# Posting one unit's small loads between two weight pieces, copying y by halves, and moving one y behind two products

## The chip, the cores and the metric

The kernel runs on one core of a Trainium2 chip. The metric is the device time of one execution in microseconds, as the median of several runs. Five engines of the core work side by side: TensorE (PE in the profile, with its weight loads as PEld), VectorE (DVE), ScalarE (ACT), GpSimd (POOL) and SyncE (SP), which here does nothing but issue DMAs, in order.

## The reference

A Mamba-2 state-space layer (4 sequences, 8 heads, 768 steps, head width 32, state width 16), and then a feed-forward layer with SiLU over its 3072 rows of 256 channels (2048 hidden):

```python
def _attn_ref(x, a, B, C):
    ...                                              # for each chunk c of the sequence
    cum = np.cumsum(la, axis=-1)                     # la = log(clip(a))
    L = np.exp(cum[:, :, :, None] - cum[:, :, None, :]) * causal
    CB = np.einsum('bhin,bhjn->bhij', Cc, Bc)
    M = CB * L
    y_intra = np.einsum('bhij,bhjd->bhid', M, xc)
    y_inter = np.einsum('bhin,bhnd->bhid', Cc, state) * decay_to_i[:, :, :, None]
    y[:, :, sl] = y_intra + y_inter
    Bx = np.einsum('bhjn,bhjd->bhjnd', Bc, xc) * decay_from_j[:, :, :, None, None]
    state = decay_full[:, :, None, None] * state + np.sum(Bx, axis=2)

def _moe_ref(x, w_in, w_out):
    h = x @ w_in
    g = h * (1.0 / (1.0 + np.exp(-h)))
    return (g @ w_out).astype(np.float32)
```

The weights `w_in` and `w_out` reach the kernel as 64-bit floats and are converted to 32 bits on the chip.

## The kernel before

The work is cut into 12 units of 256 steps (3 for each sequence). For each unit the scan makes y, which is copied to `XM`; then come the products with `w_in`, SiLU, and the products with `w_out`. Two units are taken together in the products with `w_out`, and from unit 4 on in those with `w_in` too, by a scheme that needs seven products in place of eight.

A unit needs these loads: `pa` and `ab` (two layouts of a), `tbc` (C, and for some units B, in another layout), `bn` (B) and `xt` (x). They are issued by SyncE, in this order:

```python
    def load_unit(u):
        load_pa(u, nc.sync)
        if 0 < u < UPB:
            load_n(u, 1, nc.sync)          # C of unit 1 and 2, two DMAs, 64 bytes a packet
        else:
            load_t(u, 0, nc.sync)
            load_t(u, 1, nc.sync)
        load_ab(u, nc.sync)                # four DMAs
        load_n(u, 0, nc.sync)              # B, two DMAs
        load_x(u, nc.sync)
```

The weights come in 16 pieces of 512 KB, eight of `w_in` and eight of `w_out`, through seven raw buffers. The first seven are posted at the start; `mark` is a DMA of one word that holds SyncE's queue until an earlier piece has landed:

```python
    for n in range(3):
        load_w(n, nc.sync)
    load_n(1, 0, nc.sync)
    load_n(1, 1, nc.sync)
    load_x(1, nc.sync)

    mark = const.tile([1, RAW], U32, name="mark")
    for n in range(3, RAW):                # RAW = 7
        if n > 4:
            nc.sync.dma_start(out=mark[:, n:n + 1], in_=raw[n - 2][0:1, 0, 0, 0:1])
        load_w(n, nc.sync)
```

Each piece is converted in two steps, "size" on ScalarE and "bits" on VectorE and GpSimd; the second one posts the piece seven further on:

```python
    def w_size(n):
        ...
            nc.scalar.activation(u, raw[n][:, :, :, 1].bitcast(FP32), AF.Abs)
            nc.scalar.activation(v, raw[n][:, :, :, 0], AF.Copy, scale=2.0 ** -51, bias=2.0)

    def w_bits(n, parts=1):
        ...                                # three operations on VectorE (L174, L176, L178)
                nc.gpsimd.tensor_tensor(out=dst[:, :, fs].bitcast(U32), ...)      # L182
        if n + RAW < len(W):
            load_w(n + RAW, nc.sync)
```

In the scan, `f_TP` transposes B and C of units 1 and 2 on TensorE (L355), `f_E` makes the decays E from `ab` on VectorE (L303), `f_B` multiplies B with E on GpSimd (`BT`, B-tilde, L340), `f_G` makes the products with x (L389) and CB (L404), `f_M` makes M on VectorE (L415), `f_Y` makes y on TensorE (L458, L467), and `f_X` copies it out of PSUM:

```python
    def f_X(u):
        XM[u] = xmp.tile([128, 4, 128], FP32, name="XM")
        nc.scalar.activation(XM[u], DP.pop(u)[:, :, 0:128], AF.Copy)

    def f_s1(g, j):                        # products with w_in and SiLU, for 256 hidden channels
        ...
        xm = XM[g].rearrange("p (w c) t -> p w (c t)", w=2)
        hp = ps_h.tile([128, 2, UT], FP32, name="hp")          # one of three buffers
        for i in range(2):
            f = 2 * j + i
            for kc in range(KC):           # KC = 2: the two halves of the channels of y
                nc.tensor.matmul(out=hp[:, i], lhsT=w_in_sb[:, kc, f * 128:(f + 1) * 128],
                                 rhs=xm[:, kc], start=(kc == 0), stop=(kc == KC - 1))
        nc.scalar.activation(GTS[g][:, :, j], hp, AF.Silu)
```

The order of the first units ("s6" is the size step of piece 6, "b6" its bits step; E, D, T, C, G, Y are parts of the scan of unit 2):

```python
    f_Y(0); f_Ab(1, 1); f_X(0); w_size(2); w_bits(1)
    load_unit(2)
    f_s1(0, 0)
    ...
    f_Y(1); f_X(1); w_size(5)
    f_s1(0, 3)
    steps = ((1, 0, "b5 s6"), (1, 1, "b6 s7"), (1, 2, "b7 s8"), (1, 3, "b8"), (0, 4, "E D"),
             (1, 4, ""), (0, 5, "T C s9"), (1, 5, "b9 s10"), (0, 6, "G"), (1, 6, "b10 s11"),
             (0, 7, "Y b11 s12"), (1, 7, "b12 s13"))
    for g, j, todo in steps:
        f_s1(g, j)
        w_steps(todo)
    load_unit(3)
```

And the stage in which unit 3's products with `w_in` run beside the scans of units 4 and 5 and the products with `w_out` of units 0 and 1 (`f_s2(n)`: n of these):

```python
    for j in range(8):
        f_s1(3, j)
        scan_piece(4, j, ("TE", "DCS", "G", "YS", "", "", "", ""))
        scan_piece(5, j, ("", "", "T", "E", "DCS", "G", "YS", ""))    # y of unit 5 at j = 6
        ...
        f_s2(2 if j in (5, 6) else 4)
```

Of the kernel before, what the change touches and what calls it, by code (L numbers as in the profile page):

```python
# [9 lines left out]
U32 = mybir.dt.uint32  # L10
BF16 = mybir.dt.bfloat16
AF = mybir.ActivationFunctionType
# [9 lines left out]
def kernel(  # L22
# [22 lines left out]
    nc = tc.nc  # L45
# [12 lines left out]
    const = ctx.enter_context(tc.tile_pool(name="const", bufs=1))  # L58
# [20 lines left out]
    def at(u):  # L79
        return u // UPB, u % UPB * UT  # L80

    def load_pa(u, q):

        b, t0 = at(u)
        pa[u] = loads.tile([128, UT], FP32, name="pa")
        q.dma_start(out=pa[u], in_=bass.AP(tensor=a.tensor, offset=a.offset + b * H * S + t0,
                                           ap=[[S, H], [0, N], [1, UT]]))

    def load_ab(u, q):

        b, t0 = at(u)
        ab[u] = loads2.tile([128, 2, H, Q], FP32, name="ab")
        for t in range(4):
            k, c = divmod(t, 2)
            q.dma_start(out=ab[u][64 * c:64 * c + 64, k],  # L95
                        in_=bass.AP(tensor=a.tensor, offset=a.offset + b * H * S + t0 + t * Q,
                                    ap=[[0, 64], [S, H], [1, Q]]))

    def load_n(u, i, q):

        b, t0 = at(u)
        if i == 0:
            t = bn[u] = loads.tile([128, 2, H, N], FP32, name="bn")
        else:
            t = tbc[u] = loads.tile([128, 2, 2, 8, N], FP32, name="tbc")[:, 0]
        for k in range(2):
            q.dma_start(out=t[:, k], in_=(B, C)[i][b, :, t0 + 128 * k:t0 + 128 * k + 128].rearrange("h p n -> p h n"))  # L107

    def load_t(u, i, q):

        b, t0 = at(u)
        if i == 0:
            tbc[u] = loads.tile([128, 2, 2, 8, N], FP32, name="tbc")
        for g in range(4):
            q.dma_start(out=tbc[u][32 * g:32 * g + 32, i],
                        in_=(B, C)[i][b, 2 * g:2 * g + 2, t0:t0 + UT].rearrange("e (t r) n -> t e r n", r=8))

    def load_x(u, q):
        b, t0 = at(u)
        xt[u] = loads.tile([128, 2, H, D], FP32, name="xt")  # L120
        for k in range(2):
            q.dma_start(out=xt[u][:, k], in_=x[b, :, t0 + 128 * k:t0 + 128 * k + 128].rearrange("h p d -> p h d"))

    def load_unit(u):
        load_pa(u, nc.sync)
        if 0 < u < UPB:
            load_n(u, 1, nc.sync)
        else:
            load_t(u, 0, nc.sync)
            load_t(u, 1, nc.sync)  # L130
        load_ab(u, nc.sync)
        load_n(u, 0, nc.sync)
        load_x(u, nc.sync)

    w_in_sb = const.tile([128, KC, d_ff], FP32, name="w_in_sb")
    w_out_sb = const.tile([128, NF, d_model], FP32, name="w_out_sb")
# [4 lines left out]
    RAW = 7  # L141
    raw, wu, wv = {}, {}, {}
# [7 lines left out]
    def load_w(n, q):  # L150
        src, dst = w_piece(n)
        if src.dtype == FP32:
            q.dma_start(out=dst, in_=src)
            return
        t = raw[n] = rawp.tile([128, 2, WF, 2], U32, name="raw")
        q.dma_start(out=t.rearrange("p k f two -> p k (f two)"), in_=src.bitcast(U32))
# [47 lines left out]
    load_n(1, 1, nc.sync)  # L204
    load_x(1, nc.sync)

    mark = const.tile([1, RAW], U32, name="mark")
    for n in range(3, RAW):
        if n > 4:
            nc.sync.dma_start(out=mark[:, n:n + 1], in_=raw[n - 2][0:1, 0, 0, 0:1])  # L210
        load_w(n, nc.sync)


# [57 lines left out]
    E, M, BT, BH, CT, CE, CW, PFX, ST, SM, DP, XM, GTS, BX = ({} for _ in range(14))  # L271
# [23 lines left out]
    def f_P(u):  # L295
        f_P0(u)
        f_P1(u)
# [34 lines left out]
    def f_E(u):  # L332
        f_E0(u, 0, 1)
        f_E1(u, 0, 2)
        f_E1(u, 1, 2)

    def f_B(u, engine=nc.gpsimd):

        BT[u] = sc.tile([128, 2, H, N], FP32, name="BT")
        engine.tensor_tensor(out=BT[u], in0=bn[u], in1=E[u][:, :, :, Q - 1:Q].to_broadcast([128, 2, H, N]),  # L340
                                op=ALU.mult)

    def f_T(u, i):

        t = (BH, CT)[i][u] = sc.tile([128, UT], FP32, name=("bh", "ct")[i])
        nc.vector.transpose(out=t.rearrange("p (t r) -> p r t", r=8), in_=tbc[u][:, i].rearrange("p e r n -> p r e n"))
        if i == 1:
            tbc.pop(u)

    def f_TP(u):  # L350

        tp = ps_o.tile([128, 512], FP32, name="o_ps")
        for i, t in enumerate((bn[u], tbc.pop(u))):
            for k in range(2):
                nc.tensor.transpose(out=tp[:, 256 * i + 128 * k:256 * i + 128 * k + 128],  # L355
                                    in_=t[:, k].rearrange("p h n -> p (h n)"), identity=ident)
        BH[u] = sc.tile([128, UT], FP32, name="bh")
        nc.scalar.activation(BH[u], tp[:, 0:256], AF.Copy)
        CT[u] = tp[:, 256:512]

    def f_T2(u, e):

        if e == 0:
            CE[u] = sc.tile([128, 2, UT], FP32, name="ce")
        nc.scalar.activation(CE[u][:, e], CT[u], AF.Copy, scale=par[:, e:e + 1])

    def f_C(u):

        CW[u] = sc.tile([128, UT], FP32, name="cw")
        engine = nc.vector if 0 < u < UPB else nc.gpsimd  # L370
        engine.tensor_tensor(out=CW[u].rearrange("p (c t) -> p c t", t=Q),
                             in0=CT.pop(u).rearrange("p (c t) -> p c t", t=Q), in1=PFX[u][:, :, 1:], op=ALU.mult)
# [68 lines left out]
    def f_GMD(u):  # L441
        f_G(u)
        f_S(u)
        f_SM(u)
        for k in range(2):
            f_M(u, k)
# [26 lines left out]
    def f_X(u):  # L473

        XM[u] = xmp.tile([128, 4, 128], FP32, name="XM")
        nc.scalar.activation(XM[u], DP.pop(u)[:, :, 0:128], AF.Copy)

    def new_g():

        return gpool.tile([128, NF, UT], FP32, name="gT").rearrange("p (k j) t -> p k j t", k=2)  # L480


    def f_s1(g, j):
        if j == 0:
            GTS[g] = new_g()
        xm = XM[g].rearrange("p (w c) t -> p w (c t)", w=2)
        hp = ps_h.tile([128, 2, UT], FP32, name="hp")
        for i in range(2):
            f = 2 * j + i
            for kc in range(KC):  # L490
# [3 lines that stand above are left out]
        if j == 7:  # L494
            XM.pop(g)
# [138 lines left out]
    def f_s2(n):  # L634
        for _ in range(n):
            if S2 and next(S2[0], S2) is S2:
                S2.pop(0)
                f_s2(1)
# [100 lines left out]
    def scan_piece(u, j, plan):  # L739
        for what in plan[j]:  # L740
            if what == "E":
                f_P(u)
                f_E(u)
            elif what == "T":
                if u < UPB:
                    f_TP(u)
                else:
                    f_T(u, 0)
                    f_T(u, 1)
                f_T2(u, 0)  # L750
                f_T2(u, 1)
            elif what == "t":
                f_T(u, 0)
                f_T(u, 1)
            elif what == "B":
                f_B(u)
                f_C(u)
            elif what == "D":
                f_B(u)
            elif what == "C":  # L760
                f_C(u)
            elif what == "S":
                f_SW(len(SW))
            elif what == "G":
                f_GMD(u)
            elif what == "Y":
                f_Y(u)
                f_X(u)
# [48 lines left out]
    f_X(0)  # L817
    w_size(2)
    w_bits(1)
    load_unit(2)  # L820
    f_s1(0, 0)
    f_Ek(1, 0)
    f_TP(1)
# [40 lines left out]
    def outputs(todo):  # L864
        for what in todo:
            what()
# [29 lines left out]
    for j in range(8):  # L896
        waiting, PEND[:] = PEND[:], []
        f_s1(3, j)
        scan_piece(4, j, ("TE", "DCS", "G", "YS", "", "", "", ""))
        scan_piece(5, j, ("", "", "T", "E", "DCS", "G", "YS", ""))  # L900
        scan_piece(6, j, ("",) * 7 + ("t",))
        if j == 7:
            for i in range(4):
                f_XT(2, i)

        f_s2(2 if j in (5, 6) else 4)
        if j == 3:
            f_SO(3)
        outputs(waiting)
        if j == 5:  # L910
            f_T1(1, 0)
            f_T1(1, 1)
            f_TS(1, 3, 0)
        if j in (2, 5):
            load_unit(6 + j // 3)
# [67 lines left out]
```

## Time and profile before

| | |
|---|---|
| time, median of 3 runs | 353.75 us (352.82 to 354.04) |
| profiled execution: span | 353.3 us |
| PE busy | 343.8 us, 97% of the span |
| VectorE, ScalarE, GpSimd busy | 58%, 46%, 32% |
| DMA | 42.79 MB, mean 121 GB/s |

The page's second part cuts the span into 40 slices of 8.83 us; a digit is the busy share in tenths:

```
PE   8979999999999999999999999999999999999995
DVE  6997879978586663553664563564452232234821
ACT  2567487233323645454645445544545454453100
DMA  6986895699649398958179956057404237522202
```

PE is at 9 in nearly every slice. VectorE and the DMA engines are busy early, while the weights are loaded and converted, and later have room. A busy engine in such a row does not say what the others wait for: that is read from the order of instructions in a stage. A row of the timeline gives start and length in us, the engine and the line of the kernel, what is written and read, the shape, and the count; "SPq" stands for a DMA's issue by SyncE, whose length holds any time that the issue was held up. One product in the program (32-bit, 128x256) shows as two records of PE.

### The profile page before, as it was taken

To read this page: it belongs to the slowest core of one execution; us is meant where nothing else is said; L and a number is where in the kernel's file an instruction comes from. 1 tells how busy PE (TensorE), PEld (TensorE's weight loads), DVE (VectorE), ACT (ScalarE), POOL (GpSimd) and SP (SyncE) were. 2 spreads that over 40 slices of the span, in tenths; PEclk is the share of its full clock that TensorE was granted. 3 is DMA by queue.
4 is the path that set the end of the run, shared out by engine and by line. 5 is a ranking of instruction groups with operands and counts; after the bars stand their busy time and mean duration, and the time that the engine had idled before them with its cause. 6 is when DMAs were issued, how large, how long until landed. Compare 5 with 4: busy or idle time off the path is not lost.

```text
span 353.3 us, 8349 instructions
## 1 busy us (share of the span) xinstructions
PE 343.8 (97%) x3308; PEld 287.5 (81%) x3308; DVE 204.4 (58%) x408; ACT 162.0 (46%) x394; POOL 111.5 (32%) x137
## 2 busy tenths in 40 slices
PE   8979999999999999999999999999999999999995
PEld 3658778888888888888888888888888888888883
DVE  6997879978586663553664563564652232234821
ACT  2567487233323645454645445544545454453100
POOL 4344335554085041244041244041234112051200
PEclk9999999999999999999999999999999999999999
DMA  6986895699649398958179956057404237522202
GB/s 107 225 243 161 174 371 108 125 194 210 132 99 154 81 185 164 184 104 147 32 146 185 172 98 105 16 98 143 92 2 74 51 61 142 90 46 38 36 4 46
DMA packets 117376, 42.79 MB, mean 121 GB/s; under 512 B 102488, under 2 KB 109144, under 8 KB 117336
## 3 DMA queue, kind: packets, MB, share of 16 engines
q1 hardware_dynamic: 110328, 25.67, 34.7%
q0 software_dynamic: 4464, 16.25, 24.9%
q10 hardware_dynamic: 2544, 0.33, 0.6%
q8 instruction: 26, 0.43, 0.6%
q14 instruction: 14, 0.11, 0.1%
HBM read 22.83 MB, written 3.15 MB: 74 GB/s over the span
## 4 chain that ended last, share of the span: by engine, by line
PE 75%; DVE 9%; DMA 8%; SPq 5%; issue 2%; ACT 0%; ACTq 0%; DVEq 0%
PE o_ps L627 32%; PE hp L682 28%; PE hp L491 4%; PE hp L627 3%; DMA out_dram<-ot 2%; DMA ab<-in_a_dram 2%; SPq L95 2%; PE o_ps L613 2%; PE gy L467 2%; DVE E L303 1%; DVE E L415 1%; DMA raw<-in_moe_w_out_dram 1%; SPq L107 1%; PE gy L458 1%; DMA gT<-in_a_dram 1%
## 5 line engine op out<-in xcount | busy, mean ns | idle before, releaser
L685 DVE TENSOR_TENSOR gT<-hp,p 128x256 f32<-128x256 f32 x64 | 26.9, 420 | 73.8 <-ACT p L696 37.9
L491 PE MATMUL hp<-XM,w_in_sb 128*128 128x256 f32 x256 | 59.6, 382 | 2.0 <-POOL w_in_sb L182 2.0
L627 PE MATMUL o_ps<-gT,w_out_sb 128*128 128x256 f32 x240 | 60.4, 379 | 0.0
L688 ACT ACTIVATE gT<-gT 128x256 f32<-128x256 f32 x96 | 39.7, 414 | 44.0 <-DVE gT L685 43.9
L491 PEld LDWEIGHTS hp<-XM,w_in_sb 128*128 128x128 f32 x256 | 47.9, 190 | 10.0 <-POOL w_in_sb L182 3.3
L682 PE MATMUL hp<-raw 128*128 128x256 f32 x192 | 52.7, 380 | 0.0
L544 POOL TENSOR_TENSOR ps<-ps 128x256 f32<-128x256 f32 x35 | 29.2, 835 | 72.3 <-ACT ps L574 71.0
L627 PEld LDWEIGHTS o_ps<-gT,w_out_sb 128*128 128x128 f32 x240 | 45.4, 190 | 6.3
L539 POOL DMA_DIRECT2D gT<-gT x31 | 27.4, 921 | 64.9 <-PE hp L682 22.3
L682 PEld LDWEIGHTS hp<-raw 128*128 128x128 f32 x192 | 36.2, 190 | 5.4 <-POOL ps L544 0.6
L696 ACT ACTIVATE p<-hp 128x256 f32<-128x256 f32 x64 | 24.5, 383 | 27.5 <-PE hp L682 26.1
L685 DVE TENSOR_TENSOR gT<-hp,u 128x256 f32<-128x256 f32 x32 | 13.6, 425 | 39.3 <-PE hp L682 39.3
L682 PE MATMUL hp<-XM,w_in_sb 128*128 128x256 f32 x128 | 34.1, 389 | 0.0
L493 ACT ACTIVATE gT<-hp 128x512 f32<-128x512 f32 x32 | 19.0, 594 | 28.3 <-PE hp L491 28.2
L682 PEld LDWEIGHTS hp<-XM,w_in_sb 128*128 128x128 f32 x128 | 23.3, 190 | 4.3 <-issue 1.0
L303 DVE TENSOR_TENSOR_SCAN E<-ab,diag 128x256 f32<-128x256 f32 (+1 forms) x32 | 25.6, 842 | 0.4
L574 ACT ACTIVATE ps<-o_ps 128x256 f32<-128x256 f32 x38 | 14.4, 382 | 23.9 <-PE o_ps L627 22.2
L340 POOL TENSOR_TENSOR BT<-bn,E 128x256 f32<-128x256 f32 x12 | 9.0, 748 | 50.2 <-DVE E L303 48.9
L627 PE MATMUL o_ps<-gT,wu 128*128 128x256 f32 x88 | 22.4, 380 | 0.0
L627 PE MATMUL o_ps<-gT,wv 128*128 128x256 f32 x88 | 22.2, 380 | 0.0
L627 PE MATMUL o_ps<-gT,raw 128*128 128x256 f32 x80 | 20.6, 382 | 0.0
L682 PE MATMUL hp<-raw,w_in_sb 128*128 128x256 f32 x64 | 19.1, 380 | 0.0
(125 smaller groups left out, 518.7 us busy)
## 6 DMA issues: line engine op xcount, KB each, us to landing
gT<-gT POOLq DMA_DIRECT2D x31, 512.0 KB, 6.0
ab<-in_a_dram SPq DMA_DIRECT2D x40, 128.0 KB, 3.9
raw<-in_moe_w_in_dram SPq DMA_DIRECT2D x8, 512.0 KB, 6.3
raw<-in_moe_w_out_dram SPq DMA_DIRECT2D x8, 512.0 KB, 6.5
xt<-in_x_dram SPq DMA_DIRECT2D x24, 128.0 KB, 5.7
out_dram<-ot SPq DMA_DIRECT2D x92, 32.0 KB, 2.5
bn<-in_B_dram SPq DMA_DIRECT2D x22, 64.0 KB, 4.8
tbc<-in_C_dram SPq DMA_DIRECT2D x40, 32.0 KB, 1.8
```

What stands on the lines that cost most here:

```text
L303: nc.vector.tensor_tensor_scan(out=E[u].rearrange("p k h t -> p (k h t)")[:, Q * g0:Q * (g0 + n)], data0=t.rearrange("p g t -> p (g t)"), ...
L340: engine.tensor_tensor(out=BT[u], in0=bn[u], in1=E[u][:, :, :, Q - 1:Q].to_broadcast([128, 2, H, N]), op=ALU.mult)
L491: nc.tensor.matmul(out=hp[:, i], lhsT=w_in_sb[:, kc, f * 128:(f + 1) * 128], rhs=xm[:, kc], start=(kc == 0), stop=(kc == KC - 1))
L493: nc.scalar.activation(GTS[g][:, :, j], hp, AF.Silu)
L539: nc.gpsimd.dma_start(out=o[:, js], in_=a[:, js], accum_op=ALU.add)
L544: engine.tensor_tensor(out=o, in0=p, in1=q, op=op)
L574: nc.scalar.activation(pn, on, AF.Copy)
L627: nc.tensor.matmul(out=o, lhsT=w(j), rhs=g()[:, j], start=(j == 0), stop=(j == last))
L682: nc.tensor.matmul(out=o, lhsT=w, rhs=x_, start=start, stop=True, skip_group_check=True)
L685: nc.vector.tensor_tensor(out=o, in0=p, in1=q, op=ALU.add)
L688: nc.scalar.activation(o, i, AF.Silu)
L696: nc.scalar.activation(o, i, AF.Copy)
```

## The change

Three things change. First, the loads of unit 2 are split: `pa`, C and B (`load_bc`) are posted between weight pieces 5 and 6, in place of a `mark`, and `ab` and x (`load_ax`) where all of the unit's loads stood before. It is meant to have B and C of unit 2 there before TensorE asks for them. As a consequence B stands ahead of `ab` in all units from 2 on. Second, y of units 0 and 1 is copied in two halves, so that the products with the first half of the channels may begin before the second half is copied. Third, two products with `w_out` are moved ahead of unit 5's y, so that they fill the time in which M of that unit is awaited.

```diff
-    def load_unit(u):
+    def load_bc(u):
         load_pa(u, nc.sync)
         if 0 < u < UPB:
             load_n(u, 1, nc.sync)
         else:
             load_t(u, 0, nc.sync)
             load_t(u, 1, nc.sync)
+        load_n(u, 0, nc.sync)
+
+    def load_ax(u):
         load_ab(u, nc.sync)
-        load_n(u, 0, nc.sync)
         load_x(u, nc.sync)
+
+    def load_unit(u):
+        load_bc(u)
+        load_ax(u)
...
-    mark = const.tile([1, RAW], U32, name="mark")
+    mark = const.tile([1, 1], U32, name="mark")
     for n in range(3, RAW):
-        if n > 4:
-            nc.sync.dma_start(out=mark[:, n:n + 1], in_=raw[n - 2][0:1, 0, 0, 0:1])
+        if n == 5:
+            nc.sync.dma_start(out=mark, in_=raw[3][0:1, 0, 0, 0:1])
+        if n == 6:
+            load_bc(2)
         load_w(n, nc.sync)
...
         XM[u] = xmp.tile([128, 4, 128], FP32, name="XM")
-        nc.scalar.activation(XM[u], DP.pop(u)[:, :, 0:128], AF.Copy)
+        y = DP.pop(u)
+        n = 2 if u < 2 else 4
+        for i in range(0, 4, n):
+            nc.scalar.activation(XM[u][:, i:i + n], y[:, i:i + n, 0:128], AF.Copy)
...
-    load_unit(2)
+    load_ax(2)
...
         f_s1(3, j)
+        if j == 6:
+            f_s2(2)
         scan_piece(4, j, ("TE", "DCS", "G", "YS", "", "", "", ""))
...
-        f_s2(2 if j in (5, 6) else 4)
+        f_s2((4, 4, 4, 4, 4, 2, 0, 4)[j])
```

## The prediction

> **What bounds the kernel now.** I read the page first. Section 1 puts the matmul engine at the top, and the granted clock (PEclk, 9 in all 40 slices) leaves nothing to explain there:
>
> ```profile
> PE 343.8 (97%) x3308; PEld 287.5 (81%) x3308; DVE 204.4 (58%) x408; ACT 162.0 (46%) x394; POOL 111.5 (32%) x137
> ```
>
> Second, busy time by stage (I chose the borders). The columns after the stretch's length are busy us (and instructions) of PE, PEld, DVE, ACT, POOL, then the clock, the DMA share and GB/s:
>
> ```profile
> 14.00:52.00 38.00, 35.10 (x490) 28.18 (x476) 31.45 (x54) 24.97 (x49) 15.23 (x14) 1.00 0.82 223
> 52.00:96.00 44.00, 44.00 (x433) 37.40 (x432) 35.67 (x57) 17.48 (x36) 18.76 (x17) 1.00 0.83 156
> 96.00:114.00 18.00, 17.76 (x286) 14.98 (x282) 14.39 (x22) 5.71 (x13) 11.95 (x12) 1.00 0.71 127
> 114.00:300.00 186.00, 186.00 (x1712) 158.49 (x1711) 90.81 (x214) 93.61 (x250) 52.55 (x70) 1.00 0.59 109
> ```
>
> PE has no idle time from 52 to 96 us and from 114 to 300. So nothing that the change does can shorten those stretches; at most it can keep or spoil them. What can be won lies in 14 to 52 us (38.00 - 35.10 = 2.90 us idle) and in 96 to 114 (0.24).
>
> Third, PE in order of time, around each place that the change speaks of. In brackets is the idle time ahead of a group and what ended it:
>
> ```profile
> 26.21 14.08 PE L491 MATMUL hp<-XM,w_in_sb 128*128 128x256 f32 x64 [0.73 <-POOL w_in_sb L182]
> 40.59 0.75 PE L355 MATMUL o_ps<-ident,bn 128*128 128x128 f32 x2 [0.30 <-DMA bn<-in_B_dram]
> 41.18 0.38 PE L355 MATMUL o_ps<-ident,tbc 128*128 128x128 f32 x2
> ...
> 50.15 0.69 PE L458 MATMUL gy<-cw,sm 32*64 32x64 f32 x32 [0.50 <-DVE E L415]
> ...
> 107.96 0.69 PE L458 MATMUL gy<-cw,sm 32*64 32x64 f32 x32 [0.24 <-DVE E L415]
> ```
>
> The first wait is for unit 2's B, which lands too late for the transposes; the second for unit 2's M = CB*L, the third for unit 5's. The B wait is larger than its 0.30. In unit 1 the same transposes started at 17.20 and those of C at 17.42, 0.22 us apart; here 40.59 and 41.18, 0.59 apart, because the second half of B landed later still. So 0.30 + 0.37 = 0.67 us.
>
> Fourth, the sync engine's queue, which shows why B and unit 2's M are late:
>
> ```profile
> 24.31 0.41 SPq L156 DMA_DIRECT2D raw<-in_moe_w_out_dram  x1
> 24.78 0.68 SPq L86 DMA_DIRECT2D pa<-in_a_dram  x1
> 25.50 4.97 SPq L107 DMA_DIRECT2D tbc<-in_C_dram  x2
> 30.52 5.94 SPq L95 DMA_DIRECT2D ab<-in_a_dram  x4
> 36.50 1.25 SPq L107 DMA_DIRECT2D bn<-in_B_dram  x2
> 37.79 2.82 SPq L122 DMA_DIRECT2D xt<-in_x_dram  x2
> 40.71 4.13 SPq L156 DMA_DIRECT2D raw<-in_moe_w_out_dram  x7
> ```
>
> B is issued at 36.50 because C and `ab` sit in front of it for 4.97 and 5.94 us, and the next weight piece (number 9) can't be issued before 40.71. The chain of waits then runs from that piece to the 0.50 us on PE:
>
> ```profile
> 35.82 4.50 DMA ab<-in_a_dram
> 40.71 5.00 DMA raw<-in_moe_w_out_dram
> 48.80 1.21 DVE E L415 x2
> ```
>
> Piece 9 lands at 45.71; ScalarE and VectorE convert it first (VectorE 46.49 to 47.97), and only then do unit 2's state and M come, ending at 50.01.
>
> **What the Trainium skill says.** "DMA: Bandwidth & Descriptors", section "Queues, rings and completion order": a sync-engine DMA is spread over rings, and each of the 16 engines takes descriptors in ring order. The queue above agrees: after four weight pieces (issued from 22.04 on), C's two issues take 4.97 us, where B's two take 1.25, so what is posted first is served first. The same page, "Why small descriptors are slow (HBM only)": each packet has a fixed cost. C and B come in packets of 64 bytes and the weights in pieces of 2 KB, and the page's slices from 26.5 to 44 us, where those loads run, show 161 and 174 GB/s against 371 in the slice from 44 to 53, which is weights alone for the most part. "VectorE: DVE Perf Modes", section on the TRN2 errata: a ScalarE copy out of PSUM has a fixed part beside the part per element. The trace agrees: 128x512 takes 0.60 us, 128x256 0.38, so two halves are not free.
>
> **The change part by part.**
> (1) Unit 2's `pa`, C and B are posted between pieces 5 and 6, ahead of pieces 6, 7 and 8, instead of after 8; `ab` and x stay behind 8. One gate (piece 6 waiting for piece 4 through `mark`) goes. B is then issued some ten microseconds sooner (from 36.5 to about 25 or 27) and lands well ahead of 40. Removed: 0.67 us of PE.
> (2) With 1.25 us of B gone from in front of it, and without the stretch around 33 to 35 us where the queue was stuck on `ab` and the DMA engines had nearly nothing to do (0.25 and 0.28 busy in 32 to 34 and 34 to 36), piece 9 should be issued around 38 and land around 43 instead of 45.7. VectorE then converts it by about 46, M is done near 48, and PE comes to unit 2's y at 50.15 - 0.50 - 0.67 = 48.98. Removed: 0.50. It needs M 50.01 - 48.98 = 1.0 us sooner, so piece 9 has to land at least 1.0 us sooner; I expect 2 to 3.
> (3) y of units 0 and 1 in two copies. Two copies of 128x256 come out every 0.27 us (17.89 to 18.16), so the first half is there some 0.2 us sooner, the whole some 0.06 later. But unit 0's product starts at 15.39, when the first half of weight piece 0 is converted (POOL, 14.46 to about 15.3), while the undivided copy was done at 15.13; and after unit 1's copy (25.73 to 26.33) PE does unit 0's products till about 27.9, and stood 0.73 us for weight piece 3 anyway. Nothing won, nothing lost: 0.
> (4) Unit 5's y behind two products: 4 matmul records at the 0.216 us that PE steps in this stretch (8 in 1.73 us), 0.86 us of work that was ready. It covers 0.24.
> (5) In every later unit B is posted ahead of `ab` instead of behind, so `ab` goes 1.2 us later. It matters once: unit 5's `ab` was waited for (VectorE, 0.81 us up to 98.20), on the chain that ends in the 0.24 us at 107.96. If the queue as a whole runs 2 us ahead after (2), this is paid for; if not, M of unit 5 comes up to 1.2 us later against 0.86 + 0.24 of cover.
> Sum if all goes well: 0.67 + 0.50 + 0.24 = 1.41 us. PE issues the same matmuls, so every microsecond removed reaches the end.
>
> **Rivals.**
> A. Pieces 6, 7 and 8 come late. 4096 small packets now go first. Against: PE needs piece 6 only at about 43 us and it was converted at 34.1. For: ScalarE works in order, and its size step for a piece stands ahead of a Silu that frees one of three product buffers; piece 7 was already waited for (0.45 us up to 32.74). I estimate from the order of ScalarE's work that piece 7 may land up to about 34.7 and piece 8 up to 36.4 before PE stands. Some 3 us later than now, PE loses 0.5 to 1 us and the gain is halved.
> B. The next wait takes B's place. Unit 2's B-tilde on POOL ends at 44.60, and PE came to its product at 44.94 with a third of a microsecond of slack in its weight load. If PE comes 0.67 sooner and E is not sooner, 0.3 to 0.4 of the 0.67 comes back. E began when `ab` landed at 40.4; VectorE was free at 39.7, so E can be at most 0.75 sooner unless the conversion of piece 8 moves. Likely a loss of 0 to 0.3.
> C. Step (5) without the queue's lead: 0.2 to 1.0 us back at unit 5's y.
> D. Nothing at all moves, because the DMA engines are the bound from 14 to 52 us (0.82 busy). Against: they stood for about 3 us in 32 to 36.
>
> **Range and chances.** 353.75 - 1.41 = 352.34 if everything holds; I take 0.35 off the gain as the mean of the rivals: 353.75 - 1.06 = 352.7. The three times before spread over 1.22 us, more than the gain, so the range is 351.8 to 353.9. 2% is 7 us; the whole idle time in question is 3.1 us. Faster by over 2%: 0.01; within 2%: 0.98; slower by over 2%: 0.01.
>
> **What would show it.** (1) No wait of the transposes for B near 40 us, and C's transposes 0.22 us behind B's. (2) Piece 9 issued before 39; no wait at unit 2's y near 49. (3) Unit 0's first product still held by the conversion of piece 0, at 15.4. (4) No wait at unit 5's y near 107. Rival A: a wait of ScalarE for pieces 6 to 8 between 30 and 37, followed by one of PE for a free product buffer. Rival B: PE waiting for B-tilde near 44. Rival C: VectorE waiting longer than 0.81 for unit 5's `ab`. I am wrong if PE's idle time in 14 to 114 us does not shrink by at least 0.5 us, or if idle time appears in 52 to 96 or past 114.

## The result and the profile after

| | time before | time after | ratio after/before, 95% interval |
|---|---|---|---|
| the change | 353.75 us (352.82 to 354.39, 5 runs) | 353.97 us (353.24 to 354.17, 5 runs) | 1.0006 [0.9983, 1.0029] |
| the same two kernels once more, more runs | 352.93 us (352.64 to 354.73, 53 runs) | 353.65 us (353.01 to 354.10, 15 runs) | 1.0011 [1.0003, 1.0020] |

The change was expected to take 1.06 us off. The interval of the second row says that it adds between 0.1 and 0.7 us; the two medians there are 0.72 us apart, at its upper end. The wait for B is gone, and so is the one for M of unit 2, exactly where the prediction placed them; but a wait of 1.17 us has appeared between them.

The page's section 1 of the changed kernel, engine by engine (busy us, share of the span, instructions):

```profile
PE 343.2 (98%) x3307; PEld 288.1 (82%) x3308; DVE 205.9 (59%) x408; ACT 162.3 (46%) x396; POOL 111.2 (32%) x137
```

(In the rows of the page before, slice 29 of VectorE is 6, not 4.)

Busy time by stage of the changed kernel, columns as in the prediction:

```profile
14.00:52.00 38.00, 34.82 (x476) 28.37 (x464) 33.52 (x55) 25.37 (x52) 16.25 (x14) 1.00 0.90 232
52.00:96.00 44.00, 44.00 (x466) 37.52 (x464) 34.48 (x56) 17.41 (x36) 16.88 (x16) 1.00 0.90 162
96.00:114.00 18.00, 18.00 (x267) 15.21 (x252) 14.53 (x22) 5.75 (x13) 12.94 (x13) 1.00 0.66 116
```

From 52 us to 114 PE has no idle time now, the 0.24 us of unit 5's y included. But in 14 to 52 us it is idle for 38.00 - 34.82 = 3.18 us, where it was 2.90 in the profile before. From 14 to 114 us that is 3.18 against 3.14: nothing shrank, which the prediction had named as its sign of being wrong.

PE in order of time, in the changed kernel, through unit 2's scan, and at unit 5's y:

```profile
39.95 0.38 PE L363 MATMUL o_ps<-ident,bn 128*128 128x128 f32 x2
40.17 0.38 PE L363 MATMUL o_ps<-ident,tbc 128*128 128x128 f32 x2
...
45.17 0.43 PE L397 MATMUL gy<-xt,BT 64*32 64x64 f32 x24 [1.17 <-POOL BT L348]
...
49.80 0.69 PE L466 MATMUL gy<-cw,sm 32*64 32x64 f32 x32
...
108.17 0.69 PE L466 MATMUL gy<-cw,sm 32*64 32x64 f32 x32
```

The transposes of B (39.95) and C (40.17) start 0.22 us apart and wait for nothing. Unit 2's y (49.80) waits for nothing either, and unit 5's (108.17) neither. Instead the product with B-tilde waits 1.17 us for GpSimd. This is the event that the prediction named as the sign of its second rival.

Where it comes from is read backwards, first in the sync engine's queue of the changed kernel:

```profile
22.74 1.11 SPq L107 DMA_DIRECT2D tbc<-in_C_dram  x2
23.89 2.74 SPq L107 DMA_DIRECT2D bn<-in_B_dram  x2
26.68 1.83 SPq L162 DMA_DIRECT2D raw<-in_moe_w_in_dram  x2
28.61 0.42 SPq L162 DMA_DIRECT2D raw<-in_moe_w_out_dram  x1
29.07 2.94 SPq L95 DMA_DIRECT2D ab<-in_a_dram  x4
```

C (22.74) and B (23.89) stand where they were put, ahead of pieces 6 to 8. Pieces 6 and 7 are now posted from 26.68 on and piece 8 at 28.61; piece 9 follows at 36.55, before 39, as was forecast. Then the three engines that handle piece 8 and unit 2's decays, first ScalarE (its size steps), then VectorE, then GpSimd:

```profile
31.30 0.67 ACT L170 ACTIVATE wu<-raw 128x512 f32<-128x512 f32 x1 [0.92 <-DMA raw<-in_moe_w_in_dram]
...
35.92 0.68 ACT L170 ACTIVATE wu<-raw 128x512 f32<-128x512 f32 x1 [1.27 <-DMA raw<-in_moe_w_out_dram]
```

```profile
36.63 1.20 DVE L180 TENSOR_SCALAR wu<-wu 128x512 f32<-128x512 f32 x1 [0.44 <-ACT wu L170]
...
38.21 0.68 DVE L184 SCALAR_TENSOR_TENSOR wv<-raw,wv 128x512 uint32<-128x512 uint32 x1
...
40.72 0.66 DVE L329 TENSOR_SCALAR ab<-ab 128x1024 f32<-128x1024 f32 x1
41.63 2.34 DVE L311 TENSOR_TENSOR_SCAN E<-ab,diag 128x512 f32<-128x512 f32 x2
```

```profile
44.20 0.92 POOL L348 TENSOR_TENSOR BT<-bn,E 128x256 f32<-128x256 f32 x1 [3.96 <-PE hp L503]
```

ScalarE waits 0.92 us for piece 6 and 1.27 for piece 8. VectorE, which works in order, can begin the bits step of piece 8 only at 36.63 and is through with it at 38.89 (38.21 + 0.68). All of unit 2's decays stand behind it: `pz`, the prefix scan, `ab`, E. The line of `ab` carries no wait: `ab` had landed, so no load of unit 2 holds E. E ends at 43.97, B-tilde at 45.12, and PE starts at 45.17. GpSimd's bracket names PE, which had long been done; what came last is E, on VectorE.

### The profile page after: what moved, and what is told of

Same layout as the page of the kernel before. It is cut to its first block, busy times and chain, and to the rows that moved or that the text cites. A ratio compares the mean times of both kernels' runs of the same rounds, so it can differ in the third digit from the quotient of the medians.

```text
span 351.9 us, 8352 instructions
## 1 busy us (share of the span) xinstructions
PE 343.2 (98%) x3307; PEld 288.1 (82%) x3308; DVE 205.9 (59%) x408; ACT 162.3 (46%) x396; POOL 111.2 (32%) x137
## 4 chain that ended last, share of the span: by engine, by line
PE 90%; DVE 4%; DMA 2%; issue 1%; POOL 1%; SPq 0%; ACTq 0%; ACT 0%; DVEq 0%; POOLq 0%
PE o_ps L639 36%; PE hp L694 28%; PE hp L503 15%; PE hp L639 3%; PE gy L475 2%; PE o_ps L625 2%; PE gy L412 2%; PE gy L466 2%; DMA gT<-in_a_dram 1%; PE gy L397 1%; DVE wv L184 1%; DVE E L423 1%; DVE E L311 1%; DMA tbc<-in_B_dram 1%; DVE st L438 0%
```

## The experiments

All are compared with the kernel before on the same chip.

**The two kernels again.** Each of them was profiled twice more, without an edit: e5 (before) and e6 (after) with more timed runs, e10 (before) and e11 (after) with a profile alone.

> The kernel before once more, for a second profile of it. Theory (the profile that the prediction was read from was an execution with late loads: 355.06 us against a median of 353.75): in this profile PE has no idle time for B near 40 us and none at unit 2's y near 48, unit 2's y comes about 33.4 us after unit 0's first product in place of 34.8, and the wait at unit 5's y (0.2 to 0.3 us) is there in some executions and not in others. Rival (the waits for B and M are the rule): about 0.67 and 0.5 us of idle time at the same two places again. Time: ratio 1.000.

> The changed kernel once more, beside the kernel before on the same chip. Theory (the change adds a wait of 1.1 to 1.2 us of PE for B-tilde, because piece 8 lands about 2 us later and stands ahead of E on VectorE, and takes away waits that most executions of the kernel before don't have): that wait is there again, and the time is 0.3 to 0.9 us above the kernel before, ratio 1.001 to 1.0025. Rival (the change wins what its two profiles show, 0.5 us up to the first product of units 4 and 5): ratio 0.998 to 0.999.

> One more look at the kernel before, for its waits and its end. Theory: no wait for B near 40 and none at unit 2's y, as in the second profile; the time from the last transpose on PE to the end 4.0 to 4.3 us, as in all four profiles so far with ab ahead of B. Rival (the end differs from execution to execution, whatever the kernel): 3.2 to 3.7 us.

> One more look at the changed kernel. Theory: a wait of 1.1 to 1.5 us for B-tilde again; the time from the last transpose on PE to the end 3.5 to 3.7 us, as in its two profiles so far, so that 0.5 to 0.6 us of what the wait costs comes back there. Rival (the end differs from execution to execution): 4.0 us or more.

Measured: e5 (before) 352.92 us, ratio 0.9999 [0.9991, 1.0007]; e6 (after) 353.65 us, 1.0011 [1.0003, 1.0020]; e10 (before) 353.05 us and e11 (after) 353.80 us, one run each. What matters is PE in order of time in e5, the kernel before:

```profile
39.87 0.38 PE L355 MATMUL o_ps<-ident,bn 128*128 128x128 f32 x2
...
43.85 0.43 PE L389 MATMUL gy<-xt,BT 64*32 64x64 f32 x24
...
48.49 0.69 PE L458 MATMUL gy<-cw,sm 32*64 32x64 f32 x32
...
105.99 0.69 PE L458 MATMUL gy<-cw,sm 32*64 32x64 f32 x32
```

There is no wait for B, none for unit 2's M, none for unit 5's M. All three waits that the change is meant to remove are missing, in the unchanged kernel. The same holds in e10. The stretch from 30 to 52 us says the same of e5 (first fence), where PE is busy for 22.00 of 22.00 us, as it is in e10; in e6, the changed kernel (second), it is idle for 1.40:

```profile
30.00:52.00 22.00, 22.00 (x245) 18.74 (x244) 19.83 (x31) 16.49 (x32) 9.38 (x8) 1.00 0.88 242
```

```profile
30.00:52.00 22.00, 20.60 (x238) 17.37 (x237) 17.02 (x31) 15.02 (x29) 8.66 (x7) 1.00 0.94 273
```

The profile that the prediction was read from took 355.06 us itself, against 352.82 to 354.04 in the three timed runs beside it and 352.64 to 354.73 in 53 later ones. Its queue shows in what it was special; here is the queue of e5:

```profile
24.06 0.41 SPq L156 DMA_DIRECT2D raw<-in_moe_w_out_dram  x1
...
25.25 3.81 SPq L107 DMA_DIRECT2D tbc<-in_C_dram  x2
29.10 5.46 SPq L95 DMA_DIRECT2D ab<-in_a_dram  x4
34.61 1.25 SPq L107 DMA_DIRECT2D bn<-in_B_dram  x2
...
38.34 3.73 SPq L156 DMA_DIRECT2D raw<-in_moe_w_out_dram  x7
```

C and `ab` take 3.81 and 5.46 us here, 4.97 and 5.94 there; B is issued at 34.61 instead of 36.50, piece 9 at 38.34 instead of 40.71. So the queue is 1.9 to 2.4 us further ahead in e5, and B is in time. Why the loads came late in the execution that was profiled first, no run shows.

The same queue gives the price of the change. Piece 8 was posted at 24.06 and is posted at 28.61 now, and `ab` at 29.10 and 29.07: the change holds piece 8 back by 4.55 us and brings `ab` not a moment sooner. And VectorE and GpSimd in e5:

```profile
36.83 0.68 DVE L178 SCALAR_TENSOR_TENSOR wv<-raw,wv 128x512 uint32<-128x512 uint32 x1
...
40.24 2.34 DVE L303 TENSOR_TENSOR_SCAN E<-ab,diag 128x512 f32<-128x512 f32 x2
```

```profile
42.80 0.64 POOL L340 TENSOR_TENSOR BT<-bn,E 128x256 f32<-128x256 f32 x1 [3.95 <-DVE E L303]
```

Piece 8's bits step is done at 37.51 (38.89 after the change), E starts at 40.24 (41.63), B-tilde ends at 43.44 (45.12). Its end is 1.68 us later: 1.39 from E and 0.28 because B-tilde takes 0.92 instead of 0.64. PE came to the product at 43.85 in e5, 0.41 after B-tilde; 1.68 less this slack, and less the 0.15 that the changed kernel's PE came later (44.00), leaves 1.12, beside the 1.17 seen.

**Each part alone.** e1 is the changed kernel without the halves and without the move at unit 5; e2 is the kernel before with that move alone; e3 the kernel before with the halves alone.

```diff
e1: the changed kernel, but
-        n = 2 if u < 2 else 4
-        for i in range(0, 4, n): ...
+        nc.scalar.activation(XM[u], DP.pop(u)[:, :, 0:128], AF.Copy)
...
-        if j == 6:
-            f_s2(2)
...
-        f_s2((4, 4, 4, 4, 4, 2, 0, 4)[j])
+        f_s2(2 if j in (5, 6) else 4)
e2: the kernel before, but
+        if j == 6:
+            f_s2(2)
...
-        f_s2(2 if j in (5, 6) else 4)
+        f_s2((4, 4, 4, 4, 4, 2, 0, 4)[j])
e3: the kernel before, but f_X of the changed kernel
```

> The kernel before with the split of the loads alone (pa, C and B of unit 2 between pieces 5 and 6, B ahead of ab in later units); y undivided, unit 5's y in its old place. Theory (the wait for B turns into a wait for B-tilde, because VectorE takes E of unit 2 behind piece 8, which lands about 2 us later): no wait of the transposes for B near 40, PE waits about 1.2 us for B-tilde near 44 to 45, no wait at unit 2's y, and at unit 5's y 0 to 0.1 us, because unit 5's ab is no longer waited for and M ends at about 107.1 as in the changed kernel. The first product of units 4 and 5 starts 0.2 to 0.6 us sooner after unit 0's first product than the 99.3 us of the kernel before. Rival (moving B ahead of ab makes unit 5's M late and only the two products hide it): 0.5 to 1.2 us of wait at unit 5's y. Time: 353.0 to 353.9, same.

> The kernel before with two products ahead of unit 5's y, nothing else. Theory: all as before up to 107 us (0.30 us idle for B, 0.50 at unit 2's y), the wait at unit 5's y gone, 0.24 to 0.33 us won from unit 0's first product to the first product of units 4 and 5 (99.0 in place of 99.3). Rival (y later makes XM of unit 5, and with it the first differences on GpSimd, late): a new wait at the first product with a difference, nothing won. Time: 353.4, same.

> The kernel before with y of units 0 and 1 copied by halves, nothing else. Theory: unit 0's first product is held by the conversion of weight piece 0 on GpSimd and not by the copy, so nothing moves: 99.3 us from there to the first product of units 4 and 5, the same waits as before. Rival (the copy is what holds the first product): it starts 0.15 to 0.2 us sooner. Time: 353.7, same.

Measured: e1 353.90 us, 1.0021 [1.0011, 1.0031]; e2 353.08 us, 1.0000 [0.9992, 1.0008]; e3 353.22 us, 1.0003 [0.9993, 1.0013]. PE in e1 shows the split's wait in full:

```profile
45.25 0.43 PE L397 MATMUL gy<-xt,BT 64*32 64x64 f32 x24 [1.11 <-POOL BT L348]
```

So the split of the loads makes the kernel slower, and by itself; the halves and the move are worth nothing that 14 runs can show. Against what was expected of them, e2 and e3 show no wait for B and none at unit 2's y. In e3, which lacks the move, unit 5's y waited 0.24 us, as in the profile before; in e1, e5, e7 and e10, which lack it too, it waited for nothing.

**E ahead of piece 8.** If the wait comes from E's place in VectorE's order behind the late piece, it goes when E and B-tilde go first; if it comes from the loads themselves, from `ab` or from the DMA engines, it stays. Everything else is the changed kernel:

```diff
-    steps = ((1, 0, "b5 s6"), (1, 1, "b6 s7"), (1, 2, "b7 s8"), (1, 3, "b8"), (0, 4, "E D"),
+    steps = ((1, 0, "b5 s6"), (1, 1, "b6 s7"), (1, 2, "b7 s8"), (1, 3, "E D"), (0, 4, "b8"),
```

> The changed kernel with unit 2's E and B-tilde ahead of piece 8's bits step on VectorE and GpSimd; the loads stand as in the changed kernel. Theory: E starts when ab lands at about 38.4 in place of 40.7, B-tilde ends near 42.5, the 1.2 us wait of PE for it is gone, none takes its place, and the first product of units 4 and 5 comes about 1.2 us sooner than in the changed kernel (97.6 us after unit 0's first product in place of 98.8). Time: 352.5 to 352.8. Rival (VectorE has too much to do before unit 2's y wherever E stands): the wait moves on to unit 2's y near 49, 0.5 to 1.2 us, and nothing is won.

Measured: 352.71 us, 0.9989 [0.9982, 0.9996], where e1, with the same split and timed beside it, has 353.90 and [1.0011, 1.0031]. The profile is of e4's fastest execution (352.07). Its loads, then VectorE and PE:

```profile
27.86 0.41 SPq L162 DMA_DIRECT2D raw<-in_moe_w_out_dram  x1
28.33 4.01 SPq L95 DMA_DIRECT2D ab<-in_a_dram  x4
...
35.47 0.70 ACT L170 ACTIVATE wu<-raw 128x512 f32<-128x512 f32 x1 [0.50 <-DMA raw<-in_moe_w_out_dram]
```

```profile
38.91 2.34 DVE L311 TENSOR_TENSOR_SCAN E<-ab,diag 128x512 f32<-128x512 f32 x2
41.16 0.40 DVE L180 TENSOR_SCALAR wu<-wu 128x512 f32<-128x512 f32 x1
```

```profile
43.63 0.43 PE L397 MATMUL gy<-xt,BT 64*32 64x64 f32 x24
```

E starts at 38.91, 2.7 us sooner than in the changed kernel, piece 8's bits step follows at 41.16, and PE waits for nothing. The cause is shown: piece 8 and `ab` are posted behind unit 2's C and B here too, piece 8 is used only 0.45 us sooner than in the changed kernel (35.47 against 35.92), and what differs is the order on VectorE and GpSimd. It is VectorE's that counts: in the changed kernel GpSimd was through with piece 8 at 40.23, well before E. The new order makes the split harmless, not useful: PE does this stretch no faster than in e5, which has no split.

**The end of the kernel.** One thing in the sums didn't close: the changed kernel waits 1.2 to 1.4 us more, but is only 0.1 to 0.7 us slower, and e4 is faster than the kernel before although both have no wait from 30 to 52 us. PE's starts divide each execution. Unit 0's first product starts at 14.89 to 15.44 us, whatever the kernel (15.12 in e5, 15.44 in e10). From there to unit 2's y it is 33.4 us in e2, e3, e4, e5, e7 and e10, and 34.6, 34.8 and 35.1 in three profiles of the changed kernel (the first one, e6, e11): the change costs 1.2, 1.5 and 1.8 us here. From there to the last two transposes it is 298.3 to 298.4 us in all but two, the first profile of the kernel before (298.7) and e3 (298.6). The rest of the difference lies after the last product. From the start of the last two transposes on PE to the end of the span, each the core's span less a line of PE:

| load order in units 3 and later | kernels: us |
|---|---|
| `ab` ahead of B | before 4.4, e2 4.4, e3 4.2, e5 4.5, e9 4.3, e10 4.2 |
| B ahead of `ab` | after 3.8, e1 3.5, e4 3.9, e6 3.9, e7 3.5, e8 3.9, e11 3.6 |

The means are 4.3 and 3.7 us. Two kernels test whether the order does it: e7, the kernel before with B ahead of `ab` in all units and no split, and e12, the changed kernel with the old order in units 3 and later.

```diff
e7: the kernel before, but
-        load_ab(u, nc.sync)
         load_n(u, 0, nc.sync)
+        load_ab(u, nc.sync)
e12: the changed kernel, but load_unit(u), used for units 3 and later, issues
     pa, C (or B and C in the other layout), ab, B, x   as in the kernel before
```

> The kernel before with B ahead of ab in every unit's loads, and no other change: nothing goes ahead of pieces 6 to 8. Theory (the cost lies in what the split puts ahead of piece 8, not in the swap): piece 8 lands as in the kernel before, so no wait for B-tilde above 0.2 us near 44; unit 5's ab goes 1.2 us later, so that the wait at unit 5's y is 0.3 to 1.2 us where it was 0 to 0.3. Time: 0 to 0.8 us above the kernel before. Rival (the swap makes E of unit 2 late): PE waits 0.8 to 1.2 us for B-tilde near 44, as with the split.

> The changed kernel, with the old order of loads (`ab` ahead of B) in units 3 and later, so that only unit 2 has B first. Theory: the wait for unit 2's B-tilde (1.2 to 1.4 us) comes from unit 2's loads alone and stays, and the end that is 0.5 to 0.7 us shorter comes from B standing ahead of `ab` in the later units and goes: from the last transposes of TensorE to the end of the span 3.9 to 4.2 us again (3.3 to 3.6 in the changed kernel), and the time is higher by 0.9 to 1.4 us than that of the kernel before, ratio 1.0025 to 1.0040. Rival: the end is a matter of chance, or of the split itself: the end stays at 3.3 to 3.6 and the ratio at 1.0005 to 1.0018.

Measured: e12 354.03 us, 1.0037 [1.0024, 1.0050]; e7 353.52 us (351.80 to 356.37 in 14 runs), 1.0007 [0.9990, 1.0025]. The last output is issued by ScalarE; its lines in the changed kernel (span 351.9) and in e12 (span 352.0):

```profile
349.36 0.37 ACTq L615 DMA_DIRECT2D out_dram<-ot  x1
```

```profile
348.84 0.37 ACTq L622 DMA_DIRECT2D out_dram<-ot  x1
```

From there to the end it is 2.5 us in the changed kernel and 3.2 in e12; in e5, which issues it at 348.28 of 351.4, it is 3.1. (Over all 14 profiles it is 2.5 to 2.6 with B ahead, 2.8 to 3.2 with `ab` ahead.) From the transposes e12 takes 4.6 us, no less than the kernel before (the 3.9 to 4.2 expected were counted from the second transpose, which begins 0.3 us later). So the short end goes when the old order comes back. Its wait for B-tilde was 0.68 us in this profile, less than the 1.2 to 1.4 expected, and its time is 0.8 to 1.8 us above the kernel before. e7's profile (its fastest run, 351.80 us) has no wait for B or B-tilde, none at unit 5's y, and the short end of 3.5 us; but its other runs lie 0.5 to 4.6 us higher, and no profile shows why. The wait of 0.3 to 1.2 us at unit 5's y that was expected of it did not come. Why the order of loads changes the last landing stays open.

**A version that is faster than both.** e8 is e4 with the bits steps of pieces 1 to 3 in two halves on GpSimd, because in all these kernels PE waits for these pieces between 15 and 27 us (2.0 us in the changed kernel, three waits). e9 is the control without a split: the kernel before, with those halves and the move at unit 5.

```diff
e8: e4, and e9: the kernel before with the move of e2, each with
-    w_bits(1)      w_bits(2)      w_bits(3)
+    w_bits(1, 2)   w_bits(2, 2)   w_bits(3, 2)
```

> The changed kernel with E of unit 2 ahead of piece 8's bits step, and besides with the last step of pieces 1, 2 and 3 on GpSimd in two halves, as piece 0 has it. PE waits 0.33, 0.94 and 0.74 us for these three pieces in every profile so far. Theory: a half takes 0.86 us against 1.27 for the whole, so PE may begin 0.4 us sooner each time; as VectorE paces the pieces, 0.4 to 0.8 us are won in all, ratio 0.997 to 0.998 against the kernel before. Rival ([...]the bits steps come later by as much): the waits stay as they are, ratio 0.999.

> The kernel before with two products ahead of unit 5's y and with the last step of pieces 1 to 3 in two halves on GpSimd; the loads of unit 2 stay together behind piece 8, y undivided. Theory (the split of the loads is worth nothing, with E in either place, because most executions don't wait for B): as fast as the split with E ahead of piece 8 and the halved pieces, ratio 0.9975 to 0.9985 against the kernel before, with no wait of PE near 40, 44 or 48 us above 0.35. Rival (the early post of B is what wins, once E doesn't stand behind piece 8): 0.5 us or more slower than that version, ratio 0.9995 to 1.0005.

Measured: e8 352.25 us, 0.9979 [0.9971, 0.9986], against 352.93 us before; e9 352.71 us, 0.9989 [0.9981, 0.9997], against 353.15 us. PE in e8:

```profile
25.43 14.39 PE L503 MATMUL hp<-XM,w_in_sb 128*128 128x256 f32 x64 [0.63 <-POOL w_in_sb L188]
...
48.67 0.69 PE L466 MATMUL gy<-cw,sm 32*64 32x64 f32 x32 [0.33 <-ACT gT L505]
```

The wait for piece 3 is 0.63 us where it was 0.74, and the one ahead of 21.29 is 0.55, where the largest of the three was 0.9. From unit 0's first product (15.16) to 25.43 it is 10.27 us, against 10.84 in e4: 0.57 won. But a new wait of 0.33 us stands at unit 2's y, and the 32 products (64 records) from 25.43 on take 14.39 us instead of 14.08. From unit 0's first product to unit 2's y e8 takes 33.5 us, no less than e4's 33.4. So this profile (of an execution of 352.50 us, above e8's median) does not show what makes e8 faster.

e9 shares the halved pieces and lacks both the split and the new load order. It takes 33.1 us for the same stretch, although B is only just too late in it:

```profile
39.55 0.34 PEld L355 LDWEIGHTS o_ps<-ident,bn 128*128 128x128 f32 x2 [0.34 <-DMA bn<-in_B_dram]
```

PE is 0.4 us sooner here than in e5 (25.52 against 25.95 for the first of the 32 products) and loses 0.25 us of it at these transposes. e9's end is 0.4 us longer than e8's (4.3 against 3.9). Its ratio lies between what its theory (0.9975 to 0.9985) and its rival (0.9995 to 1.0005) had said, and the intervals of e8 and e9 overlap, so which of the two is faster is not shown. Nothing here shows that the split is worth anything: by these two profiles it spares 0.25 us at B and costs more than that further on.

## Why the prediction was wrong

The prediction was 352.7 us, 1.06 below the kernel before, with a range up to 353.9; the result lies 0.22 us above the kernel before, just outside the range and on the wrong side of the change. By its steps:

1. **0.67 us for unit 2's B: failed.** The mechanism was read rightly (the transposes of B start 0.22 us ahead of C's now, nothing waits), but the size belongs to the one execution that was profiled. In e5, e10 and in e2 and e3, whose loads are the same, it is 0; in e9, whose PE comes 0.4 us sooner, it is 0.25.
2. **0.50 us at unit 2's y: failed, in the same way.** It is 0 in those four too. The queue's lead over the profile before exists in both kernels: e5, without the change, issues piece 9 at 38.34 us, where 40.71 was the starting point.
3. **Halves of y, 0: right.** e3 gives 1.0003 [0.9993, 1.0013].
4. **0.24 us at unit 5's y: not there as a rule.** The move covers the wait where it occurs; e5 and e10 have none, e3 had 0.24, and e2 gives 1.0000 [0.9992, 1.0008].
5. **B ahead of `ab` in the later units:** feared for up to 1.2 us at unit 5's y (rival C). Neither the changed kernel nor e7 waits there. What it did do was not foreseen: the end is 0.6 us shorter. "Every microsecond removed reaches the end" took that end as fixed.

The rivals: **A** was right in its cause and in its limits, and small in its effect. ScalarE did wait for pieces 6 and 8 (in e6 for 7 too), and began piece 8 at 35.92, 36.43 and 36.41 us in three profiles of the changed kernel (the first one, e6, e11); the limit that the prediction gave was 36.4. In the first two PE lacked no product buffer. In e11 PE had come to these 32 products at 25.86, 0.35 us sooner than in the profile that the limit was read from (26.21), and there it did stand. PE, ScalarE, and PE's weight loads in e11:

```profile
25.86 14.39 PE L503 MATMUL hp<-XM,w_in_sb 128*128 128x256 f32 x64 [0.74 <-POOL w_in_sb L188]
```

```profile
36.41 0.67 ACT L170 ACTIVATE wu<-raw 128x512 f32<-128x512 f32 x1 [1.31 <-DMA raw<-in_moe_w_out_dram]
36.99 0.66 ACT L172 ACTIVATE wv<-raw 128x512 f32<-128x512 uint32 x1
37.56 1.54 ACT L505 ACTIVATE gT<-hp 128x512 f32<-128x512 f32 x3
```

```profile
38.25 1.59 PEld L503 LDWEIGHTS hp<-XM,w_in_sb 128*128 128x128 f32 x8 [0.44 <-POOL w_in_sb L188]
```

Three Silus stand behind piece 8 at 37.56. The first takes 0.58 us and ends at 38.14; PE's weight loads, held for 0.44 us, go on at 38.25, and the 32 products take 0.31 us longer than the 14.08 of e6. (The bracket names GpSimd, which had been through with the weight piece of these products, number 5, since 30.99; the Silu is what came last.) e8, whose PE comes sooner still (25.43), loses the same 0.31.

**B** was right in its effect, and 0 to 0.3 us is the mis-sized term: it is 1.17, 1.40 and 1.41 us in three profiles of the changed kernel.

The two were put down as separate rivals, and the step between them was written down and not followed: "E can be at most 0.75 sooner unless the conversion of piece 8 moves". It does move, by the change itself, and to the later side. I asked of the late pieces only what ScalarE does behind them, and not what VectorE does.

**C** did not come (step 5). **D**, that nothing moves, did not either: B came sooner and piece 8 later.

So the step that failed is the sum: its gains of 0.67, 0.50 and 0.24 us are not there in a second profile, and rival B's 0 to 0.3 is 1.2 to 1.4. With 0.3 for the product buffer in e11 and about -0.6 for the end, the changed kernel should be 0.6 to 1.1 us slower, beside a measured 0.1 to 0.7. The two upper values are from executions above the median (354.10 and 353.80 us against 353.65). For e1 the same sum gives 1.1 - 0.8 = 0.3 us (its end is 3.5 us), beside a measured 0.4 to 1.1: too little, and what is missing was not found.

## What to carry to other kernels

Before a wait of half a microsecond is worth a change, see whether it is in a second profile of the same kernel, and whether the profiled execution's own time is a usual one; here it was slower than each of 53 others, and two further profiles of the kernel had none of its three waits. When a transfer is moved forward in a queue that works in order, list what it pushes back, and for each of these what stands behind it on every engine that handles it: the loss came two steps on, in work that shares nothing with the load but VectorE's order. If such a transfer must come late, put the work that the bounding engine waits for ahead of its conversion, as e4 does with one swap.

## What the runs showed of the hardware

The order of the loads in the middle of the kernel changes its last 4 us: 4.3 us in the mean with `ab` ahead of B, 3.7 with B ahead, over 13 profiles without an overlap (4.2 to 4.5 against 3.5 to 3.9), and 4.6 when the old order was put back. The larger part is the landing of the last output after its issue (2.8 to 3.2 against 2.5 to 2.6 us). No run shows the mechanism.

VectorE and GpSimd lengthen each other's work. The first operation of piece 8's bits step takes 0.40 us in e4, and 1.20 in the changed kernel, where it runs beside GpSimd's step of piece 7 (36.27 to 37.55):

```profile
36.27 1.28 POOL L188 TENSOR_TENSOR w_in_sb<-wu,wv 128x512 uint32<-128x512 uint32 x1 [1.42 <-DVE wv L184]
```

The Trainium skill, "SBUF — State Buffer", section "SBUF: two separate sides", says that GpSimd and some operations of VectorE (those in a two-port mode, or with two inputs in SBUF) share a pair of ports as an exclusive lock, and that the one that starts first holds it for its whole instruction. The trace agrees as far as it goes: GpSimd's step starts first, and VectorE's operation ends 0.28 us after it (37.83 against 37.55). In e5 B-tilde starts first (42.80) and takes 0.64 us, and VectorE's operation beside it takes 0.88; in the changed kernel both start at 44.20, VectorE's takes 0.42 and B-tilde 0.92. Which mode these operations run in, no run shows.
